# State products in four quarters of TensorE's array, a ScalarE pass moved behind the Squares, and a new order of the first steps

## The chip, the cores and the metric

One core of one Trainium2 chip. The metric is the device time of one execution in microseconds, the median of the runs. The engines that matter here are TensorE (PE in the views, its weight loads PEld), VectorE (DVE), ScalarE (ACT) and the DMA queue that SyncE (SP) feeds.

## The reference

Attention with a decaying state (retention), then two feed-forward layers. q, k, v are (4, 8, 768, 64) in float32; the weights are float64, 512 x 2048 and 2048 x 512 twice.

```python
gamma = 1.0 - 2.0 ** (-5.0 - np.arange(H))
for t in range(S):
    state = gamma * state + k[:, :, t] (outer) v[:, :, t]
    y[:, :, t] = (q[:, :, t] @ state) / sqrt(D)
x = y with heads joined                      # (3072, 512)
h = x @ moe_w_in;   x = (h - tanh(h)) @ moe_w_out
h = x @ moe2_w_in;  out = where(h > 0, h, exp(min(h, 0)) - 1) @ moe2_w_out
```

## The kernel before

**Attention.** The sequence is cut into 6 chunks of 128 positions for each of 4 batches: 24 attention steps s, chunk s // 4 of batch s % 4. Eight heads are four pairs p of two heads j; a head has 64 rows. One attention step has scores (`att_scores`, L164: for each head k against q, 64 rows by 128 columns, j = 0 and j = 1 into two banks, a0 and a1), a mask on VectorE (L172) that gives pt, and a scaling of q in place (`att_scale_q`, L135). Its output (`att_out`) is, for each head, the carried state with the scaled q (the state product, L192: 64 rows by 64 columns) plus v with pt (L200: 128 rows by 64 columns). Both add up in one bank, a0, where head j = 0 of a pair takes partitions 0 to 63 and j = 1 takes 64 to 127. ScalarE copies the output to the high half of x (L208), VectorE subtracts that from the output for the low half (L209). The state's update (`att_state`, `state_mm`, L219: scaled k with v, in bank a1) is added by VectorE (L242, L245). The k for it is scaled on VectorE (`att_scale_k`, L149). The first four attention steps have no state behind them; their updates are copied (L233).

**Feed-forward.** Each product is made of three TensorE passes of high and low halves. The loop runs over steps n = 0 to 191: a block of 512 tokens b and a slice f of 128 of the 2048 inner columns. A step has 12 matmuls into h (`first_mm`, L256), the activation (`act_tanhshrink`, `act_elu`), and 12 matmuls into four accumulators (`second_mm`, L322) for the step two before it (SKEW = 2). An attention step's scores come behind `first_mm` of one step, its output and state behind that of the next; their copies and additions are taken up at the start of the step after that. Those of attention step 5 come at n = 1 and n = 2, of 6 at 3 and 4, of 7 at 5 and 6, and so on, later ones further apart.

**Activation.** On ScalarE: two Squares (L276, L277), `between()`, that is, the hand-over of the previous step's g (`flush`, `split_hi`, L265), Tanh (L279) and Relu (L280). On VectorE four operations (L282, L285, L288, L289), interleaved with a list `side`: the low half of g (L269), masks, and weight passes.

**Weights.** Each float64 tile of 128 x 512 is fetched raw (`fetch`, L81) and made into two float32 halves: `convert_a` on ScalarE (L86) writes a staging tile, one of four (pool `stg`); `convert_b` on VectorE (L93, L94) puts in the missing bits; `convert_c` copies the high half on ScalarE (L106) and subtracts it on VectorE (L107), which frees the staging tile. `todo[n]` names the tiles whose `convert_b` stands in step n; two for each of the first five steps, then one.

The order on every engine is the order in which the program is written (`manual_schedule`); each engine works through its list in turn. Before the loop, a hand-written list of first steps starts the first four attention steps, the first two weight tiles and the scores of attention step 4.

Of the kernel before, what the change touches and what calls it, by code (L numbers as in the profile page):

```python
# [40 lines left out]
def retention_moe_kernel(ctx: ExitStack, tc: tile.TileContext, dims, ins, out):  # L41
# [139 lines left out]

    def att_out(s):
        t, v, _ = qkv_t[s]
        pt = pt_t.pop(s)
        pool, tag = bank(s, "o")
        o = pool.tile([P, NP, P], F32, tag=tag, name=f"o{s}")
        b, c = divmod(s, B)
        if b:
            for p in range(NP):
                for j in range(2):  # L190
                    r = slice(j * D, (j + 1) * D)
                    nc.tensor.matmul(  # L192
                        out=o[r, p, :], lhsT=st[c][r, p, :], rhs=t[r, 0, p * P:(p + 1) * P],
                        start=(p == 0), stop=False, skip_group_check=True,
                    )
        for p in range(NP):
            for j in range(2):
                r = slice(j * D, (j + 1) * D)
                h = 2 * p + j
                nc.tensor.matmul(  # L200
                    out=o[r, p, :], lhsT=v[:, h * D:(h + 1) * D], rhs=pt[:, j, p, :],
                    start=(b == 0), stop=True, skip_group_check=True,
                )
        if c == 0:
            xhl[b] = xp.tile([P, 2, KC, TB], F32R, tag=f"x{b % 2}", name=f"x{b}")
        yield
        sl = slice(c * P, (c + 1) * P)
        nc.scalar.activation(out=xhl[b][:, 0, :, sl], in_=o, func=AF.Copy)  # L208
        nc.vector.tensor_tensor(  # L209
            out=xhl[b][:, 1, :, sl], in0=o, in1=xhl[b][:, 0, :, sl].bitcast(F32), op=ALU.subtract  # L210
        )

    def state_mm(ds, s):
        _, v, kn = qkv_t.pop(s)
        for p in range(NP):
            for j in range(2):
                r = slice(j * D, (j + 1) * D)
                h = 2 * p + j
                nc.tensor.matmul(  # L219
                    out=ds[r, p, :], lhsT=kn[:, h * D:(h + 1) * D], rhs=v[:, h * D:(h + 1) * D],  # L220
                    start=True, stop=True,
                )
# [12 lines left out]
    def att_state(s):  # L235
        if s // B == NCH - 1:
            return
        ds = ps_a.tile([P, NP, D], F32, tag="a1", name=f"ds{s}")
# [138 lines left out]
    def run(g):  # L377
        for _ in g:
            pass
# [4 lines left out]
    with tc.manual_schedule():  # L384
# [41 lines left out]
        def out_pe(s):  # L426
            g_out[s] = att_out(s)
            next(g_out[s])
# [7 lines left out]
        def ops(lst):  # L436
            for op in lst:
                op()
# [7 lines left out]
        convert_a(jobs0[0])  # L446
        run(g_sc[1])
        scores_pe(2)
        run(g_out[0])
        out_pe(1)  # L450
        ops(convert_b(jobs0[0]))
        run(g_sc[2])
        lo0 = convert_c(jobs0[0])
        run(g_out[1])
        scores_pe(3)
        out_pe(2)
        lo0()
        run(g_sc[3])
        run(g_out[2])
        out_pe(3)  # L460
        att_scale_k(0)
        att_scale_k(1)
        run(g_out[3])
        convert_a(jobs0[1])
        att_scale_k(2)
        att_scale_k(3)
# [4 lines left out]
        lo1 = convert_c(jobs0[1])  # L471
# [3 lines left out]
        lo1()  # L475
# [5 lines left out]
        convert_a(jobs0[3])  # L481
        ops(convert_b(jobs0[2]))
        ops(masks4)
        att_scale_k(B)
        ops(convert_b(jobs0[3]))
# [47 lines left out]
        for job in todo[0]:  # L533
            convert_a(job)
# [4 lines left out]
        def flush():  # L539
            if prev_v is not None:  # L540
                g_t[n - 1] = split_hi(prev_v, n - 1)

# [17 lines left out]
        for ph, b, f, flo, fhi in order:  # L560
# [24 lines left out]
            for job in todo.get(n + 1, []):  # L585
                convert_a(job)
# [17 lines left out]
            n += 1  # L604
        flush()
# [62 lines left out]
```

## Time and profile before

| | |
|---|---|
| median of 3 runs | 1172.61 us (1171.87 to 1172.62) |
| the profiled execution, its own time | 1170.16 us |
| its span, first to last instruction | 1168.3 us |
| TensorE busy | 1151.0 us, 99% |
| VectorE busy | 681.2 us, 58% |
| ScalarE busy | 624.1 us, 53% |
| mean granted TensorE clock | 0.995 |

The span is what the trace shows; the execution's own time has some 2 us more around it. A busy share is a mean over the whole span, so it says nothing of a stage: the views by stretch do. In the views an instruction has its line, its engine, what it writes and reads by the program's names, and behind it in brackets how long its engine had been idle and what ended that.

### The profile page before, as it was taken

The numbers are of one execution on the slowest core, as the hardware profiler recorded it, in microseconds if no ns is written. First come the engines' busy times: TensorE is split into PE (matmuls) and PEld (weight loads), VectorE is DVE, ScalarE is ACT, GpSimd is POOL, SyncE is SP. The second block draws the span as 40 slices with busy tenths as digits, with TensorE's granted clock in tenths as the row PEclk, the third lists the DMA queues.
The fourth block names the chain that finished last, engine by engine and source line by source line (L and its number), as shares of the span: only waits on it lengthen the run. The fifth ranks groups of instructions, "written<-read, shape, count | busy, mean of one in ns | idle before, by whom it ended". The sixth has DMA issues, their size and how long they took to land.

```text
span 1168.3 us, 15675 instructions
## 1 busy us (share of the span) xinstructions
PE 1151.0 (99%) x6033; PEld 941.6 (81%) x6033; DVE 681.2 (58%) x1133; ACT 624.1 (53%) x1097; POOL 5.6 (0%) x10
## 2 busy tenths in 40 slices
PE   8799999999999999999999999999999999999998
PEld 5578888888888888888888888888888888888886
DVE  6898887666666666565799766333343343343332
ACT  2657785454455445445788665453443544544434
POOL 0000000000000000000000000000000000000000
PEclk9899999999999999999999999999999999999999
DMA  9930032421103102100565300200200200200000
GB/s 338 415 140 37 1 109 42 139 52 57 37 1 108 37 28 74 45 1 18 191 227 178 108 1 1 72 1 1 73 1 1 73 1 1 73 1 1 36 1 36
DMA packets 27562, 80.44 MB, mean 69 GB/s; under 512 B 3168, under 2 KB 3168, under 8 KB 27488
## 3 DMA queue, kind: packets, MB, share of 16 engines
q1 hardware_dynamic: 26048, 76.56, 18.7%
q0 software_dynamic: 864, 2.10, 1.2%
q8 instruction: 47, 0.77, 0.3%
q10 hardware_dynamic: 576, 0.79, 0.2%
q14 instruction: 27, 0.22, 0.1%
HBM read 64.76 MB, written 14.68 MB: 68 GB/s over the span
## 4 chain that ended last, share of the span: by engine, by line
PE 93%; DVE 3%; ACT 1%; DMA 1%; issue 1%; SPq 0%; DVEq 0%; ACTq 0%
PE acc L322 44%; PE h L256 43%; PE sc L164 2%; PE o L200 2%; PE o L192 1%; PE ds L219 1%; DVE w L94 1%; DMA raw<-w 1%; DVE w L107 1%; DMA stage<-qkv 0%; DVE x L209 0%; DVE v L289 0%; DVE v L285 0%; ACT w L86 0%; DVE h L288 0%
## 5 line engine op out<-in xcount | busy, mean ns | idle before, releaser
L322 PE MATMUL acc<-g,w 128*128 128x512 f32 x1152 | 282.6, 394 | 0.0
L256 PE MATMUL h<-x,w 128*128 128x512 f32 x1152 | 278.6, 391 | 0.0
L322 PE MATMUL acc<-w,g 128*128 128x512 f32 x1152 | 276.7, 389 | 0.6 <-DVE g L269 0.6
L256 PE MATMUL h<-y,w 128*128 128x512 f32 x1152 | 276.7, 389 | 0.0
L256 PEld LDWEIGHTS h<-x,w 128*128 128x128 f32 x1152 | 217.1, 189 | 45.5 <-ACT w L106 0.2
L322 PEld LDWEIGHTS acc<-w,g 128*128 128x128 f32 x1152 | 216.1, 188 | 45.9 <-DVE g L269 1.0
L256 PEld LDWEIGHTS h<-y,w 128*128 128x128 f32 x1152 | 216.2, 188 | 44.9
L322 PEld LDWEIGHTS acc<-g,w 128*128 128x128 f32 x1152 | 213.9, 188 | 47.5 <-ACT g L265 0.7
L302 DVE SCALAR_TENSOR_TENSOR v<-v,t 128x512 f32<-128x512 f32 x96 | 66.5, 693 | 299.6 <-ACT t L300 299.6
L297 ACT ACTIVATE u<-h 128x512 f32<-128x512 f32 x96 | 57.4, 598 | 259.8 <-PE h L256 258.3
L276 ACT ACTIVATE u<-h 128x512 f32<-128x512 f32 x96 | 57.5, 599 | 224.7 <-issue 216.0
L282 DVE SCALAR_TENSOR_TENSOR v<-v,u 128x512 f32<-128x512 f32 x96 | 66.4, 692 | 152.7 <-ACT v L277 152.6
L269 DVE TENSOR_TENSOR g<-v,g 128x512 fp32r<-128x512 f32 x192 | 131.4, 685 | 0.8 <-ACT g L265 0.8
L265 ACT ACTIVATE g<-v 128x512 fp32r<-128x512 f32 x192 | 118.0, 615 | 2.0 <-DVE v L305 2.0
L289 DVE COPY_PREDICATED v<-m,h 128x512 f32<-128x512 uint16 x96 | 70.4, 734 | 4.5
L277 ACT ACTIVATE v<-u,qa_b 128x512 f32<-128x512 f32 x96 | 69.4, 723 | 3.2
L280 ACT ACTIVATE m<-u,xs_b 128x512 bf16<-128x512 f32 x96 | 68.1, 710 | 0.0
L288 DVE TENSOR_TENSOR h<-h,t 128x512 f32<-128x512 f32 x96 | 66.5, 692 | 0.0
L305 DVE TENSOR_TENSOR v<-h,v 128x512 f32<-128x512 f32 x96 | 65.6, 683 | 0.0
L285 DVE SCALAR_TENSOR_TENSOR v<-v,h 128x512 f32<-128x512 f32 x96 | 65.4, 681 | 0.0
L298 ACT ACTIVATE v<-u 128x512 f32<-128x512 f32 x96 | 60.7, 632 | 3.1
L300 ACT ACTIVATE t<-u 128x512 f32<-128x512 f32 x96 | 59.2, 617 | 0.0
(44 smaller groups left out, 601.6 us busy)
## 6 DMA issues: line engine op xcount, KB each, us to landing
raw<-w SPq DMA_DIRECT2D x64, 512.0 KB, 5.6
qk<-qkv SPq DMA_DIRECT2D x20, 512.0 KB, 5.3
v<-qkv SPq DMA_DIRECT2D x24, 256.0 KB, 5.8
x<-x1d SPq DMA_DIRECT2D x12, 512.0 KB, 5.8
kn<-qkv SPq DMA_DIRECT2D x20, 256.0 KB, 5.9
out<-o SPq DMA_DIRECT2D x10, 512.0 KB, 2.9
x1d<-o SPq DMA_DIRECT2D x8, 512.0 KB, 3.3
stage<-qkv SPq DMA_DIRECT2D x4, 512.0 KB, 6.8
```

The lines of the kernel that those rows point to most:

```text
L256: nc.tensor.matmul(out=h, lhsT=w[:, a, c * P:(c + 1) * P], rhs=x[:, b, c, :], start=(i == 0), stop=(i == 3 * KC - 1),)
L265: nc.scalar.activation(out=t[:, 0, :], in_=g, func=AF.Copy)
L269: nc.vector.tensor_tensor(out=t[:, 1, :], in0=g, in1=t[:, 0, :].bitcast(F32), op=ALU.subtract)
L277: nc.scalar.activation(out=v, in_=u, func=AF.Square, bias=qa_b)
L280: nc.scalar.activation(out=big, in_=u, func=AF.Relu, bias=xs_b)
L282: lambda: nc.vector.scalar_tensor_tensor(out=v, in0=v, scalar=QB, in1=u, op0=ALU.add, op1=ALU.mult),
L285: lambda: nc.vector.scalar_tensor_tensor(out=v, in0=v, scalar=C2, in1=h, op0=ALU.mult, op1=ALU.mult),
L288: lambda: nc.vector.tensor_tensor(out=h, in0=h, in1=th, op=ALU.subtract),
L289: lambda: nc.vector.copy_predicated(out=v, mask=big.bitcast(U16), data=h),
L302: lambda: nc.vector.scalar_tensor_tensor(out=v, in0=v, scalar=1.0, in1=th, op0=ALU.add, op1=ALU.mult),
L305: lambda: nc.vector.tensor_tensor(out=v, in0=h, in1=v, op=ALU.max),
L322: nc.tensor.matmul(out=acc[e], lhsT=lhsT, rhs=rhs, start=(f == lo and i == 0), stop=(f == hi - 1 and i == 2),)
```

## The change

It does three things. The state products of an odd pair p go to the other half of the partitions of the output (`half`), so that heads change places there, and the output has two tiles, even pairs in bank a0 and odd pairs in a1, with the update of the state in the rest of a1; the copies to x are made for each tile, and the rows of the first weight are exchanged on the host to match. `convert_a` is called inside `between()`, behind the hand-over of g, and for the tiles of the same step; it was called at the end of the step before. And the list of first steps has another order.

```diff
--- before.py
+++ after.py
@@ -179,36 +179,54 @@
         else:
             yield masks + [lambda: att_scale_q(s)]
 
+    def half(p, j):
+
+
+        j = (j + p) % 2
+        return slice(j * D, (j + 1) * D)
+
+    ds_t = {}
+
     def att_out(s):
         t, v, _ = qkv_t[s]
         pt = pt_t.pop(s)
-        pool, tag = bank(s, "o")
-        o = pool.tile([P, NP, P], F32, tag=tag, name=f"o{s}")
         b, c = divmod(s, B)
-        if b:
+        if b == 0:
+            pool, tag = bank(s, "o")
+            o = pool.tile([P, NP, P], F32, tag=tag, name=f"o{s}")
+            outs = [o[:, p, :] for p in range(NP)]
+            parts = [(slice(0, NP), o)]
+        else:
+            even = ps_a.tile([P, NP // 2, P], F32, tag="a0", name=f"oe{s}")
+            odd = ps_a.tile([P, NP, P], F32, tag="a1", name=f"oo{s}")
+            ds_t[s] = odd[:, NP // 2:, :].rearrange("p a (b d) -> p (a b) d", d=D)
+            outs = [(even, odd)[p % 2][:, p // 2, :] for p in range(NP)]
+            parts = [(slice(0, NP, 2), even), (slice(1, NP, 2), odd[:, 0:NP // 2, :])]
             for p in range(NP):
                 for j in range(2):
                     r = slice(j * D, (j + 1) * D)
                     nc.tensor.matmul(
-                        out=o[r, p, :], lhsT=st[c][r, p, :], rhs=t[r, 0, p * P:(p + 1) * P],
-                        start=(p == 0), stop=False, skip_group_check=True,
+                        out=outs[p][half(p, j)], lhsT=st[c][r, p, :], rhs=t[r, 0, p * P:(p + 1) * P],
+                        start=(p < 2), stop=False, skip_group_check=True,
                     )
         for p in range(NP):
             for j in range(2):
-                r = slice(j * D, (j + 1) * D)
                 h = 2 * p + j
                 nc.tensor.matmul(
-                    out=o[r, p, :], lhsT=v[:, h * D:(h + 1) * D], rhs=pt[:, j, p, :],
+                    out=outs[p][half(p, j)], lhsT=v[:, h * D:(h + 1) * D], rhs=pt[:, j, p, :],
                     start=(b == 0), stop=True, skip_group_check=True,
                 )
         if c == 0:
             xhl[b] = xp.tile([P, 2, KC, TB], F32R, tag=f"x{b % 2}", name=f"x{b}")
         yield
         sl = slice(c * P, (c + 1) * P)
-        nc.scalar.activation(out=xhl[b][:, 0, :, sl], in_=o, func=AF.Copy)
-        nc.vector.tensor_tensor(
-            out=xhl[b][:, 1, :, sl], in0=o, in1=xhl[b][:, 0, :, sl].bitcast(F32), op=ALU.subtract
-        )
+        x = xhl[b]
+        for k, o in parts:
+            nc.scalar.activation(out=x[:, 0, k, sl], in_=o, func=AF.Copy)
+        for k, o in parts:
+            nc.vector.tensor_tensor(
+                out=x[:, 1, k, sl], in0=o, in1=x[:, 0, k, sl].bitcast(F32), op=ALU.subtract
+            )
 
     def state_mm(ds, s):
         _, v, kn = qkv_t.pop(s)
@@ -218,7 +236,7 @@
                 h = 2 * p + j
                 nc.tensor.matmul(
                     out=ds[r, p, :], lhsT=kn[:, h * D:(h + 1) * D], rhs=v[:, h * D:(h + 1) * D],
-                    start=True, stop=True,
+                    start=True, stop=True, skip_group_check=True,
                 )
 
     def att_state_pair(j):
@@ -235,7 +253,7 @@
     def att_state(s):
         if s // B == NCH - 1:
             return
-        ds = ps_a.tile([P, NP, D], F32, tag="a1", name=f"ds{s}")
+        ds = ds_t.pop(s)
         state_mm(ds, s)
         c = s % B
         yield
@@ -443,45 +461,44 @@
         warm(3)
         run(g_sc[0])
         out_pe(0)
-        convert_a(jobs0[0])
         run(g_sc[1])
         scores_pe(2)
         run(g_out[0])
+        convert_a(jobs0[0])
         out_pe(1)
+        run(g_sc[2])
+        scores_pe(3)
+        run(g_out[1])
+        out_pe(2)
+        run(g_sc[3])
         ops(convert_b(jobs0[0]))
-        run(g_sc[2])
-        lo0 = convert_c(jobs0[0])
-        run(g_out[1])
-        scores_pe(3)
-        out_pe(2)
-        lo0()
-        run(g_sc[3])
         run(g_out[2])
         out_pe(3)
+        lo0 = convert_c(jobs0[0])
         att_scale_k(0)
-        att_scale_k(1)
         run(g_out[3])
+        lo0()
         convert_a(jobs0[1])
-        att_scale_k(2)
-        att_scale_k(3)
+        for s in range(1, B):
+            att_scale_k(s)
         pairs = [att_state_pair(j) for j in range(2)]
         for g in pairs:
             next(g)
         ops(convert_b(jobs0[1]))
-        lo1 = convert_c(jobs0[1])
         convert_a(jobs0[2])
         for g in pairs:
             run(g)
-        lo1()
+        lo1 = convert_c(jobs0[1])
         att_load_v(B)
         att_load_kn(B)
         for job in jobs0[4:12]:
             fetch(*job)
         masks4 = next(att_scores(B))
-        convert_a(jobs0[3])
         ops(convert_b(jobs0[2]))
+        lo1()
         ops(masks4)
         att_scale_k(B)
+        convert_a(jobs0[3])
         ops(convert_b(jobs0[3]))
 
 
@@ -530,8 +547,6 @@
 
         pend = []
         prev_jobs = jobs0[2:4]
-        for job in todo[0]:
-            convert_a(job)
         load_step(load.pop(-1))
         gens = []
         prev_v = None
@@ -539,6 +554,8 @@
         def flush():
             if prev_v is not None:
                 g_t[n - 1] = split_hi(prev_v, n - 1)
+            for job in jobs:
+                convert_a(job)
 
         def second(upto):
             while len(pend) > upto:
@@ -582,8 +599,6 @@
             interleave(chain, side)
             if n in scale_k:
                 att_scale_k(scale_k[n])
-            for job in todo.get(n + 1, []):
-                convert_a(job)
             prev_v = v
             prev_jobs = jobs
             pend.append((2 * ph + 1, f, n, b, flo, fhi))
@@ -602,6 +617,7 @@
                 if 8 <= f < 8 + KC:
                     split_x1(nxt, f - 8)
             n += 1
+        assert not jobs
         flush()
         split_lo(g_t[n - 1], prev_v)
         second(0)
@@ -632,6 +648,9 @@
     }
     for m, w in enumerate((moe_w_in, moe_w_out, moe2_w_in, moe2_w_out)):
         w = np.asarray(w)
+        if m == 0:
+            w = w.reshape(KC, 2, P // 2, DFF).copy()
+            w[1::2] = w[1::2, ::-1].copy()
         if m % 2 == 0:
             w = w.reshape(KC, P, NF, P).transpose(2, 1, 0, 3).reshape(NF, P, KC * P)
         else:
```

On TensorE, at step n = 2, the output of attention step 5 (o5 is its tile, oe5 and oo5 are the tiles of even and odd pairs), between `first_mm` and `second_mm`. Before:

```order
L256 MATMUL h0_2_506<-x0_190,w0_2_413 128x512 x12
L192 MATMUL o5_519<-qk5_357,st0_284 64x128 x8
L200 MATMUL o5_519<-pt5_454,v5_431 64x128 x8
L219 MATMUL ds5_536<-v5_431,kn5_359 64x64 x8
L322 MATMUL acc0_0_574<-g0_471,w1_0_415 128x512 x3
```

And now:

```order
L274 MATMUL h0_2_504<-x0_190,w0_2_413 128x512 x12
L208 MATMUL oe5_517<-qk5_353,st0_284 64x128 x2
L208 MATMUL oo5_518<-qk5_353,st0_284 64x128 x2
L208 MATMUL oe5_517<-qk5_353,st0_284 64x128 x2
L208 MATMUL oo5_518<-qk5_353,st0_284 64x128 x2
L215 MATMUL oe5_517<-pt5_452,v5_427 64x128 x2
L215 MATMUL oo5_518<-pt5_452,v5_427 64x128 x2
L215 MATMUL oe5_517<-pt5_452,v5_427 64x128 x2
L215 MATMUL oo5_518<-pt5_452,v5_427 64x128 x2
L237 MATMUL oo5_518<-v5_427,kn5_355 64x64 x8
L340 MATMUL acc0_0_572<-g0_469,w1_0_415 128x512 x3
```

The eight state products keep their place and their number; they now go by twos to either tile, and so do the products with v.

On ScalarE, step n = 2 and the start of n = 3: u, v, g, t and m are tiles of the activation, w32 the staging tiles, w the weights, x the input of the first layer. Before:

```order
L86 ACTIVATE w32_0_5_494<-raw0_5_324 128x512
L86 ACTIVATE w32_1_3_496<-raw1_3_326 128x512
L276 ACTIVATE u2_545<-h0_2_506 128x512
L277 ACTIVATE v2_547<-u2_545,qa_b_91 128x512
L265 ACTIVATE g1_551<-v1_467 128x512
L279 ACTIVATE t2_546<-h0_2_506 128x512
L280 ACTIVATE m2_548<-u2_545,xs_b_92 128x512
L106 ACTIVATE w0_4_555<-w32_0_4_427 128x512
L106 ACTIVATE w1_2_557<-w32_1_2_429 128x512
L86 ACTIVATE w32_0_6_570<-raw0_6_328 128x512
L86 ACTIVATE w32_1_4_572<-raw1_4_330 128x512
L208 ACTIVATE x1_395<-o5_519 128x4x128
L276 ACTIVATE u3_624<-h0_3_600 128x512
```

And now:

```order
L294 ACTIVATE u2_543<-h0_2_504 128x512
L295 ACTIVATE v2_545<-u2_543,qa_b_91 128x512
L283 ACTIVATE g1_549<-v1_465 128x512
L86 ACTIVATE w32_0_5_551<-raw0_5_323 128x512
L86 ACTIVATE w32_1_3_553<-raw1_3_325 128x512
L297 ACTIVATE t2_544<-h0_2_504 128x512
L298 ACTIVATE m2_546<-u2_543,xs_b_92 128x512
L106 ACTIVATE w0_4_557<-w32_0_4_471 128x512
L106 ACTIVATE w1_2_559<-w32_1_2_473 128x512
L225 ACTIVATE x1_392<-oe5_517 128x2x128
L225 ACTIVATE x1_392<-oo5_518 128x2x128
L294 ACTIVATE u3_624<-h0_3_600 128x512
```

The two passes over raw weights stood ahead of the output's copy (o5) and of the first Square of step 3; now the passes of step 2 stand behind the hand-over of g and ahead of Tanh, and the copy, now in two, stands behind the high halves of step 1's weights.

On VectorE, in the list of first steps: pt are masked scores of attention steps 0 to 3, w32_0_0 is the first weight tile. Before:

```order
L209 TENSOR_TENSOR x0_190<-o0_181,x0_190 128x4x128
L93 TENSOR_SCALAR w32_0_0_191<-w32_0_0_191 128x512
L94 SCALAR_TENSOR_TENSOR w32_0_0_191<-raw0_0_128,w32_0_0_191 128x512
L172 TENSOR_TENSOR pt2_195<-sc2_0_196,dtab_88 128x512
L172 TENSOR_TENSOR pt2_195<-sc2_1_197,dtab_88 128x512
L209 TENSOR_TENSOR x0_190<-o1_208,x0_190 128x4x128
L107 TENSOR_TENSOR w0_0_221<-w32_0_0_191,w0_0_221 128x512
L172 TENSOR_TENSOR pt3_225<-sc3_0_226,dtab_88 128x512
L172 TENSOR_TENSOR pt3_225<-sc3_1_227,dtab_88 128x512
L209 TENSOR_TENSOR x0_190<-o2_236,x0_190 128x4x128
L149 TENSOR_TENSOR kn0_137<-kn0_137,ktab_89 128x512
L149 TENSOR_TENSOR kn1_139<-kn1_139,ktab_89 128x512
```

And now:

```order
L227 TENSOR_TENSOR x0_190<-o0_181,x0_190 128x4x128
L172 TENSOR_TENSOR pt2_193<-sc2_0_194,dtab_88 128x512
L172 TENSOR_TENSOR pt2_193<-sc2_1_195,dtab_88 128x512
L227 TENSOR_TENSOR x0_190<-o1_208,x0_190 128x4x128
L172 TENSOR_TENSOR pt3_219<-sc3_0_220,dtab_88 128x512
L172 TENSOR_TENSOR pt3_219<-sc3_1_221,dtab_88 128x512
L93 TENSOR_SCALAR w32_0_0_206<-w32_0_0_206 128x512
L94 SCALAR_TENSOR_TENSOR w32_0_0_206<-raw0_0_128,w32_0_0_206 128x512
L227 TENSOR_TENSOR x0_190<-o2_232,x0_190 128x4x128
L149 TENSOR_TENSOR kn0_137<-kn0_137,ktab_89 128x512
L227 TENSOR_TENSOR x0_190<-o3_247,x0_190 128x4x128
L107 TENSOR_TENSOR w0_0_256<-w32_0_0_206,w0_0_256 128x512
```

The two bit operations of the first weight tile stood ahead of the masks of attention step 2; now they stand behind those of step 3, and the tile's last pass behind the fourth output.

## Rows read from the trace of the kernel before

**Rows 1.** Waits, whole run, TensorE: who waited, for whom, us in total, times, longest.
```profile
PE sc L164 <- DVE x L209: 7.4, 3, 3.5
...
PE acc L322 <- DVE g L269: 0.6, 1, 0.6
```

**Rows 2.** Busy us (instructions) of PE, PEld, DVE, ACT, POOL by stretch; PEclk, DMA share, GB/s.
```profile
26.40:77.50 51.10, 42.91 (x302) 33.90 (x301) 44.47 (x81) 30.20 (x53) 0.00 (x0) 0.90 0.84 339
77.50:1168.30 1090.80, 1086.69 (x5509) 893.78 (x5508) 621.35 (x1026) 586.56 (x1034) 5.42 (x6) 1.00 0.16 50
...
37.80:44.60 6.80, 6.13 (x24) 4.94 (x25) 6.70 (x13) 3.69 (x7) 0.00 (x0) 0.50 1.03 414
...
72.00:76.30 4.30, 3.19 (x14) 2.19 (x13) 3.57 (x8) 2.68 (x5) 0.00 (x0) 1.00 0.00 0
```

**Rows 3.** Waits of VectorE and ScalarE from 26.4 to 77.5 us.
```profile
DVE v L282 <- ACT v L277: 3.2, 3, 1.4
DVE x L209 <- ACT x L208: 3.0, 3, 1.2
...
ACT w L86 <- DVE w L107: 19.0, 5, 5.1
```

**Rows 4.** Timeline of step 1: start us, us, engine, line, operation, idle before and its end.
```profile
35.88 1.26 ACT L86 ACTIVATE w<-raw 128x512 f32<-128x512 f32 x2 [2.92 <-DVE w L107]
37.04 0.58 ACT L208 ACTIVATE x<-o 128x512 fp32r<-128x512 f32 x1
...
37.66 0.69 DVE L209 TENSOR_TENSOR x<-o,x 128x512 fp32r<-128x512 f32 x1 [1.21 <-ACT x L208]
...
38.40 2.93 PE L164 MATMUL sc<-qk 64*128 64x128 f32 x16 [3.51 <-DVE x L209]
```

**Rows 5.** Timeline, VectorE, steps 0 to 5: the other idle spells.
```profile
30.86 0.69 DVE L282 SCALAR_TENSOR_TENSOR v<-v,u 128x512 f32<-128x512 f32 x1 [0.45 <-ACT v L277]
...
49.13 0.69 DVE L282 SCALAR_TENSOR_TENSOR v<-v,u 128x512 f32<-128x512 f32 x1 [1.39 <-ACT v L277]
...
74.77 0.69 DVE L209 TENSOR_TENSOR x<-o,x 128x512 fp32r<-128x512 f32 x1 [0.63 <-ACT x L208]
```

**Rows 6.** Timeline, TensorE and VectorE, start of the program.
```profile
13.70 1.16 PE L164 MATMUL sc<-stage 64*128 64x128 f32 x16 [0.55 <-DMA stage<-qkv]
...
14.44 0.42 DVE L93 TENSOR_SCALAR w<-w 128x512 uint32<-128x512 uint32 x1
...
14.79 1.09 PE L200 MATMUL o<-pt,v 128*64 128x128 f32 x16
...
26.86 1.28 DVE L172 TENSOR_TENSOR pt<-sc,dtab 128x512 f32<-128x512 f32 x2
```

**Rows 7.** Groups by line, whole run: count, busy us, mean ns of one.
```profile
L245 DVE TENSOR_TENSOR st<-ds,st 128x256 f32<-128x256 f32 x16 | 6.8, 425 | 1.7
```

**Rows 8.** SyncE's load of step 1's q and k: timeline row, and its landing.
```profile
27.50 0.33 SPq L125 DMA_DIRECT2D qk<-qkv  x1
...
DMA to landing us min/median/max: 10.4/10.4/10.4
```

**Rows 9.** Timeline, TensorE: small products, dense stage first, then the start.
```profile
179.69 1.09 PE L192 MATMUL o<-qk,st 64*64 64x128 f32 x16
180.71 1.09 PE L200 MATMUL o<-pt,v 128*64 128x128 f32 x16
...
224.79 0.43 PE L192 MATMUL o<-qk,st 64*64 64x128 f32 x4
...
18.77 0.43 PE L200 MATMUL o<-pt,v 128*64 128x128 f32 x2 [0.77 <-DVE pt L172]
19.37 1.09 PE L200 MATMUL o<-pt,v 128*64 128x128 f32 x14 [0.16 <-DVE pt L172]
20.57 1.29 PE L219 MATMUL dsp<-v,kn 128*64 128x64 f32 x32
```

**Rows 10.** Groups by line, TensorE, from 77.5 us on.
```profile
L192 PE MATMUL o<-qk,st 64*64 64x128 f32 x272 | 18.5, 275 | 0.0
```

## Prediction

> **What bounds it now.** Read the waits of TensorE first: over the whole run it waits 7.4 us, three times, for VectorE's copy of an attention output (L209), and after 77.5 us only once, 0.6 us [rows 1]. Then the busy times by stretch: from 77.5 us to the end TensorE is busy for 1086.69 of 1090.80 us, while VectorE and ScalarE have 621.35 and 586.56 us of work there; from 26.4 to 77.5 us it is busy for 42.91 of 51.10 us [rows 2]. So there are two stages. In the late one a microsecond taken off TensorE's own work is a microsecond of the end; a microsecond of ScalarE or VectorE is nothing. In the early one (steps n = 0 to 5) TensorE waits, and the question is for whom.
>
> The waits of that stretch say: VectorE idles 3.2 us for the second Square (L277) and 3.0 us for the copy L208, three times each; ScalarE idles 19.0 us in `convert_a` (L86) for VectorE's last pass over an older weight tile (L107), whose staging buffer it wants [rows 3]. The timeline of step 1 shows the ring: L86 starts at 35.88 us after 2.92 us of waiting for L107, L208 stands behind it at 37.04, L209 waits 1.21 us for that, and the scores of TensorE wait 3.51 us for L209 [rows 4]. VectorE is otherwise packed there, so TensorE arrives where VectorE's queue lets it: VectorE's idle time is what can be won.
>
> **The change, part by part.**
>
> *`convert_a` behind the second Square.* It takes L86 from in front of L208 and of the Squares and puts it, with the hand-over of g, ahead of Tanh and Relu. VectorE's idle spells are 0.45 (step 0), 1.21 (step 1), 1.39 (step 2), 1.21 (step 3, a row like that of step 1), 1.39 (step 4, like step 2) and 0.63 us (step 5): 6.2 us in all, as the totals say [rows 3 to 5]. The 0.45 stays: there the Squares wait for TensorE's h, not for L86. The other 5.8 should go, because L107 is no longer waited for ahead of L208 and of the Squares. What is late next: Tanh, now behind L86. I followed step 2 through the new queues with these durations: L107 of the buffer's last owner ends about 45.8 us, the two L86 at 47.1, Tanh at 47.6; VectorE wants Tanh about 49.2, so 1.6 us cover it. In steps 3 and 5 the second Square would end within 0.1 us of when VectorE asks for it; each may give back 0.2 us or so. In the late stage L86 is covered by the skew of two steps between a weight tile's passes and its use.
>
> *The order of the first steps.* VectorE does the same operations up to the copies of the first states, in another order. Before, the two bit operations of the first weight tile (the first at 14.44 us) fill a time in which the next mask could not run yet: its scores start at 13.70 and take 1.16 us [rows 6]. After, they stand behind the fourth mask. VectorE then waits about 0.45 us for those scores and 0.5 us for ScalarE's copy of the second output (its products start at 14.79 and take 1.09 us; a copy takes 0.58 [rows 4]), and catches up part of it later. Stepped through, the masks of the fifth attention step start at about 27.6 instead of 26.86 us [rows 6]: a loss of 0.7 us. Bounds: 0, if the waits are absorbed, and 1.0, if none is. The queues of SyncE and GpSimd keep their order; no DMA is moved past another.
>
> *The outputs in two halves.* Each later attention step copies two half tiles twice instead of one tile. A 256-wide VectorE operation takes 425 ns against 0.69 us for L209 [rows 4, 7]; two cost 0.16 us more by that, about 0.08 as they overlap in the queue. Three stand ahead of the last early wait: 0.2 us. In the late stage nothing, there is room on both engines [rows 2].
>
> *Step 1.* Its scores also need q and k of that step, issued at 27.50 us and landing 10.4 us later, at 37.9 [rows 8]. In the new chain the first bank is free at about 37.5 and the second (state added) at 38.6, so the load ends that wait first and TensorE still idles some 2.6 us. The granted clock was 0.50 (1.2 GHz) over the stretch 37.8 to 44.6 us, from within the 3.51 us of idling on, and full (2.4 GHz) over 72.0 to 76.3 us, with 1.11 us of idling [rows 2, 4]; 2.6 lies between. If it falls, scores and h of step 1 and 2 take up to twice as long, some 3 us; VectorE's queue (packed until about 47 us) hides all but about 0.5. I take 0 and keep 0.5 for the range.
>
> Early sum: 5.8 - 0.7 - 0.2 = **4.9 us** (3.5 to 5.8 with the bounds). The outputs of steps 0, 2 and 4 win nothing more there by faster products: what follows them waits for VectorE's k (L149).
>
> *State products in four quarters.* An attention output has eight products of a state (L192), each in two passes: 16 matmuls in 1.09 us; four take 0.43, so a pair more costs (1.09 - 0.43)/6 = 0.11 us [rows 9]: two run side by side, rows 0-63 to columns 0-63 and rows 64-127 to 64-127. The change sends odd products to the other half of the columns and to another bank, so that all four quarters have work. No row shows four at once. For it: products that share all rows but not the columns (L200) keep the same 1.09 us for 16, and products that share columns but not rows (L164) 1.16 [rows 6], so neither sharing slows a pair. And a product need not wait for its turn: where the mask held up the second product, two passes ran alone in 0.43 us, and the 14 left then took 1.09 us, as long as 16 do: eight slots, six of two and two of one, since the left half had three products to go and the right one four [rows 9]. The halves keep queues of their own; with quarters this gives 4 slots instead of 8, 4 x 0.11 = 0.44, less 0.01 for two more starts: **0.43 us**. Bounds: 0, if no more than two ever run; 0.24, if matmuls can't come closer than L219's 32 in 1.29 us, 0.04 each, so that a slot of four takes 0.16 (8 x 0.11 - 4 x 0.16) [rows 9]; above, 0.44. I take 0.43, since each kind of sharing has its row. There are 272/16 = 17 outputs after 77.5 us [rows 10], all in the dense stage: 17 x 0.43 = **7.3 us**. The products with v (L200) come in the column order 0, 1, 1, 0; by the same queues they keep eight slots. States' updates (L219) are unchanged but for their bank.
>
> The Trainium skill, "TensorE: Matmul & The Clock Gate" (Part 3, "What overlaps and what doesn't"), says that a weight load overlaps a running matmul only where the row group differs, and that matmuls start strictly in order. By that a quarter that shares rows with a running one waits, the term is 0, and the time is that of the first rival below. This trace disagrees: L200's two column halves share all rows and pair as L192's do, and the 14 matmuls above passed a second pass that was still waiting [rows 9].
>
> Sum: 4.9 + 7.3 = 12.2 us. The profiled execution took 1170.16 us, so 1158.0 on its account; the median of the runs is 1172.61, 2.45 higher, and the prediction is made for that: **1160.4 us**.
>
> **The rivals.**
> *No more than two at once.* Everything else as above: 1172.6 - 4.9 = 1167.7 us. For it: no row of four. Against: the rows of either sharing, and of the separate queues.
> *The early win is lost.* Another wait takes the place of the ring, Tanh behind L86, or the 2.6 us of idling and a clock at 1.2 GHz through step 2 and on, and VectorE's idle time stays: 1172.6 - 7.3 = 1165.3 us. For it: the margins of 0.1 us in steps 3 and 5. Against: 1.6 us at Tanh.
> *Slower: quarters that take turns.* If two row halves writing the same columns into two banks, with two column halves reading the same rows, make each matmul run alone, 16 slots replace 8: 0.88 us more for each of 17 outputs, 15.0, less the early 4.9: 1182.7 us. It decides from 4.9/17 = 0.29 us an output. For it: no row has both sharings together. Against: each alone costs nothing.
>
> **How the numbers follow.** Forecast 0.62, two at once 0.18, early win lost 0.12, turns 0.05, and 0.03 for both gains near nothing, within 0.2%. A measurement can tell about 0.2%, 2.3 us, from no change; the first three lie beyond it. Faster 0.90 (some of the first three may shrink below it, so not 0.92), same 0.04, slower 0.06. The range: the forecast's own goes from 1172.6 - 5.8 - 7.5 = 1159.3, less 2.45 for the lower account of the profiled execution, about 1157, to 1172.6 - 3.5 - 17 x 0.24 = 1165.0; up to 1168.5 it takes in the second rival and most of the first. Outside are the turns, and the first rival where the early win is small too.
>
> **What would show it.** State products: 16 in about 0.65 us instead of 1.09, and the products with v 0.6 instead of 1.02 us after their start. No wait of L86 for L107 ahead of the copy, VectorE's waits in the early stretch about 1 us instead of 6.2. TensorE still idles some 8 us there, now also for q and k of its attention steps (L135, L149), at full clock. The scores of step 5 done by about 72.5 us (before: 77.5, where the dense stage begins). First h products 0.7 us later than before. Wrong if state products keep 1.09 us, if the scores of step 5 end after 75, or if TensorE waits anywhere after them.

## The result and the profile after

The change takes 1162.25 us (median, 1160.70 to 1164.14), the kernel before 1172.24 (1170.98 to 1172.62): a ratio of 0.9918 [0.9904, 0.9932], 10.0 us less. The forecast was 12.2 us less, at 1160.4. The profiled execution of the change took 1164.14 us, the slowest of its runs; that of the kernel before took 1170.16, 2 us below its median. The two traces are therefore 6.0 us apart where the medians are 10.0 apart, and what they lack is in the early stage.

The lines of the kernel have moved: in the change the Squares are L294 and L295, Tanh is L297, and VectorE's four operations of the activation are L300, L303, L306 and L307 (before: L282, L285, L288, L289); the copies of an output are L225 and L227, the products L208, L215, L237, and the states L251 and L263. In the runs with Tanh first, further down, the four operations stand one line lower still.

TensorE's waits over the whole run, for [rows 1] (who waited, for whom, us in total, times, longest):

```profile
PE sc L164 <- DVE x L227: 4.4, 3, 3.0
PE sc L164 <- DMA stage<-qkv: 3.7, 3, 2.1
PE dsp L237 <- DVE kn L149: 2.4, 2, 1.3
...
PE sc L164 <- DVE st L263: 2.0, 3, 0.7
...
PE oo L237 <- DVE kn L149: 1.0, 2, 0.6
...
PE acc L340 <- DVE g L287: 0.6, 1, 0.6
```

The stages, cut where the last early scores end (77.96 us; 77.46 before), for [rows 2], and two stretches of the early one in which the granted clock was 0.50 (1.2 GHz):

```profile
26.40:77.96 51.56, 44.18 (x326) 34.50 (x322) 47.12 (x88) 30.54 (x57) 0.00 (x0) 0.88 0.89 348
77.96:1162.40 1084.44, 1079.63 (x5509) 886.55 (x5508) 624.64 (x1043) 588.69 (x1052) 5.42 (x6) 1.00 0.16 50
...
24.90:31.70 6.80, 6.51 (x57) 5.61 (x54) 6.64 (x12) 1.19 (x2) 0.00 (x0) 0.50 0.92 349
41.90:48.70 6.80, 6.22 (x25) 4.96 (x26) 6.73 (x14) 2.28 (x5) 0.00 (x0) 0.50 1.04 418
```

The dense stage went from 1090.84 us (77.46 to 1168.30) to 1084.44, 6.4 less; by the medians that leaves 3.6 us for the early stage, where 4.9 was forecast. In this execution the early stage even ends 0.5 us later than before: what the ring (L86 waiting for L107's staging tile) had cost is gone, and something else took it up. VectorE's waits from 26.4 to 78 us, for [rows 3]:

```profile
DVE v L303 <- ACT t L297: 2.1, 4, 0.7
DVE v L300 <- ACT v L295: 2.1, 1, 2.1
```

The 19.0 us of L86 for L107 and the 3.0 us of the copies are gone, and so are the waits for the second Square except one, in step 0. In their place VectorE's second operation of the activation (L303) waits for Tanh. Step 2 shows how (start us, us, engine, line, operation, idle before and its end):

```profile
51.58 1.23 ACT L86 ACTIVATE w<-raw 128x512 f32<-128x512 f32 x2
...
52.71 0.58 ACT L297 ACTIVATE t<-h 128x512 f32<-128x512 f32 x1
...
53.32 0.69 DVE L303 SCALAR_TENSOR_TENSOR v<-v,h 128x512 f32<-128x512 f32 x1 [0.70 <-ACT t L297]
```

L303 doesn't use Tanh's result; it reads h, which Tanh reads too, and the program has it wait until Tanh is done (53.29 us). Tanh now stands behind the two raw passes.

The first output of the dense stage, for [rows 9], on TensorE:

```profile
83.64 0.33 PE L208 MATMUL oe<-qk,st 64*64 64x128 f32 x2
83.66 0.33 PE L208 MATMUL oo<-qk,st 64*64 64x128 f32 x2
83.80 0.28 PE L208 MATMUL oe<-qk,st 64*64 64x128 f32 x2
83.82 0.28 PE L208 MATMUL oo<-qk,st 64*64 64x128 f32 x2
...
84.02 0.28 PE L208 MATMUL oe<-qk,st 64*64 64x128 f32 x2
84.03 0.28 PE L208 MATMUL oo<-qk,st 64*64 64x128 f32 x2
84.24 0.33 PE L215 MATMUL oe<-pt,v 128*64 128x128 f32 x2
```

Four quarters run at once: two to `oe` and two to `oo` start within 20 ns, and each next four 0.11 to 0.16 us behind. The products with v follow 0.60 us after the first state product, in all 20 outputs 597 or 598 ns; before it was 1020 or 1021. That is 0.423 us an output, and 17 outputs make 7.2 us. The dense stage gained 0.8 us less than that, most of it at one place: the state's update of attention step 8 now comes before its k is scaled (the view ends behind the twelfth of its 16 matmuls).

```profile
182.14 0.57 PE L237 MATMUL oo<-v,kn 128*64 128x64 f32 x12 [0.48 <-DVE kn L149]
```

So the quarters did what was forecast. What fell short is for the most part in the early stage, and the experiments take the three parts of the change apart.

### The profile page after: what moved, and what is told of

Read it like the earlier page. It is cut to its first block, busy times and chain, and to the rows that moved or that the text cites. A ratio compares the mean times of both kernels' runs of the same rounds, so it can differ in the third digit from the quotient of the medians.

```text
span 1162.4 us, 15704 instructions
## 1 busy us (share of the span) xinstructions
PE 1142.7 (98%) x6033; PEld 934.3 (80%) x6033; DVE 684.9 (59%) x1153; ACT 625.2 (54%) x1117; POOL 5.6 (0%) x10
## 4 chain that ended last, share of the span: by engine, by line
PE 94%; DVE 3%; DMA 2%; issue 0%; SPq 0%; ACT 0%; DVEq 0%; ACTq 0%
PE acc L340 45%; PE h L274 44%; PE sc L164 2%; PE oe L215 1%; PE oe L208 1%; PE oo L237 1%; PE oo L215 1%; DMA raw<-w 1%; DMA stage<-qkv 1%; DVE w L94 1%; DMA dtab<-dtab 1%; DVE w L107 1%; DVE kn L149 0%; DVE v L307 0%; SPq L81 0%
## 5 line engine op out<-in xcount | busy, mean ns | idle before, releaser
L274 PE MATMUL h<-x,w 128*128 128x512 f32 x1152 | 279.7, 392 | 0.0
L274 PE MATMUL h<-y,w 128*128 128x512 f32 x1152 | 276.7, 389 | 0.0
L274 PEld LDWEIGHTS h<-x,w 128*128 128x128 f32 x1152 | 218.0, 190 | 45.9 <-issue 0.4
L274 PEld LDWEIGHTS h<-y,w 128*128 128x128 f32 x1152 | 216.2, 188 | 44.9
L294 ACT ACTIVATE u<-h 128x512 f32<-128x512 f32 x96 | 57.6, 600 | 236.8 <-issue 224.8
L300 DVE SCALAR_TENSOR_TENSOR v<-v,u 128x512 f32<-128x512 f32 x96 | 66.4, 692 | 137.1 <-ACT v L295 137.1
L307 DVE COPY_PREDICATED v<-m,h 128x512 f32<-128x512 uint16 x96 | 70.4, 733 | 4.5
L303 DVE SCALAR_TENSOR_TENSOR v<-v,h 128x512 f32<-128x512 f32 x96 | 65.6, 683 | 10.0 <-ACT t L297 10.0
L295 ACT ACTIVATE v<-u,qa_b 128x512 f32<-128x512 f32 x96 | 69.5, 724 | 3.1
L306 DVE TENSOR_TENSOR h<-h,t 128x512 f32<-128x512 f32 x96 | 66.5, 692 | 0.0
```

The lines of the kernel that those rows point to most:

```text
L274: nc.tensor.matmul(out=h, lhsT=w[:, a, c * P:(c + 1) * P], rhs=x[:, b, c, :], start=(i == 0), stop=(i == 3 * KC - 1),)
L295: nc.scalar.activation(out=v, in_=u, func=AF.Square, bias=qa_b)
L300: lambda: nc.vector.scalar_tensor_tensor(out=v, in0=v, scalar=QB, in1=u, op0=ALU.add, op1=ALU.mult),
L303: lambda: nc.vector.scalar_tensor_tensor(out=v, in0=v, scalar=C2, in1=h, op0=ALU.mult, op1=ALU.mult),
L306: lambda: nc.vector.tensor_tensor(out=h, in0=h, in1=th, op=ALU.subtract),
L307: lambda: nc.vector.copy_predicated(out=v, mask=big.bitcast(U16), data=h),
```

## The experiments

Each time is a median with the lowest and highest run; "before" is the kernel before, run beside it on the same chip. "The list" is the hand-written order of the first steps.

### One part at a time

**The quarters alone.** The change, with the raw passes back in their old place and the old list of first steps:

```diff
-            for job in jobs:
-                convert_a(job)
...
+            for job in todo.get(n + 1, []):
+                convert_a(job)
```

> The kernel before with the state products in quarters, the two output tiles and the halved copies alone; passes over raw weights and the order of the first steps as before. Theory: the quarters account for 0.42 us of each of the 17 outputs in the dense stage, and nothing of the early stage moves: 7.2 us less than before, about 1165.0 us, products with v 0.60 us behind the state products' start. Rival (the quarters' gain is partly given back by the second pair of copies on VectorE, which is full in the early stage): 6 us less or worse, and the last scores of the early stage later than 77.5 us.

1164.51 us (1163.65 to 1166.67), before 1172.11: 0.9942 [0.9929, 0.9954], 7.6 less; the term was 7.3. VectorE's early waits are still those behind L86, for the Square and for the copy (2.35 of the 5.1 us are in step 0, where L86 waits for its raw tile and not for L107):

```profile
DVE v L300 <- ACT v L295: 5.1, 3, 2.3
DVE x L227 <- ACT x L225: 2.4, 3, 1.0
```

**The raw passes alone**, in the kernel before:

```diff
             g_t[n - 1] = split_hi(prev_v, n - 1)
+            for job in jobs:
+                convert_a(job)
...
-            for job in todo.get(n + 1, []):
-                convert_a(job)
```

> The kernel before with the passes over raw weights behind the hand-over of g alone. Theory: the ring of waits goes (5.8 us of VectorE's idle time), but Tanh, now behind two raw passes, is late for VectorE's second operation of the activation, which reads h as Tanh does: about 2 us come back, so 3 to 4 us less than before, about 1168.6 us, VectorE waiting for Tanh some 2 us before 78 us. Rival (the early win was lost to the first steps' order and the clock, not to Tanh): 5 us less or more, about 1167 us. Second rival (nothing is won, the ring's waits only change their name): within 1 us of before.

1166.84 us (1166.21 to 1168.71), 0.9963 [0.995, 0.9975], 5.3 less; the term was up to 5.8. The expectation that Tanh would take some 2 us back missed, and its rival (5 us less or more) came out: the 2.7 us that VectorE waits for Tanh here are not lost to the end one for one. The ring is gone, and Tanh is there:

```profile
DVE v L285 <- ACT t L279: 2.7, 4, 1.2
DVE pt L172 <- PE sc L164: 1.7, 1, 1.7
DVE v L282 <- ACT v L277: 0.6, 2, 0.5
```

**The start order alone**, in the kernel before: the hand-written list of the change, nothing else.

```diff
         out_pe(0)
-        convert_a(jobs0[0])
...
         run(g_out[0])
+        convert_a(jobs0[0])
...
         run(g_sc[3])
+        ops(convert_b(jobs0[0]))
```

> The kernel before with the new order of the first steps alone. Theory of the prediction: VectorE reaches the masks of the fifth attention step 0.7 us later, and since VectorE is full until step 5, the end is 0.7 us later: 1172.9 us. Rival (the new order lets TensorE idle longer ahead of the third scores, and a clock at 1.2 GHz adds to that): 2 to 3.5 us slower, 1174 to 1176 us, first h products after 28 us. Second rival (the new order helps, as the copies come earlier): up to 1 us faster.

1172.62 us (1170.80 to 1174.43), 1.0004 [0.9995, 1.0013]: 0.5 us slower, no difference that can be told from none (the interval goes from 0.6 us faster to 1.5 slower).

**All but the start order**: the change with the old list.

> The changed kernel with the old order of the first steps (quarters and raw passes remain). Theory: 7.2 from the quarters and 3 to 4 from the raw passes: about 1161.5 us, 0.7 less than the changed kernel. Rival (the new order of the first steps took 3 us): about 1159 us. Second rival (the order does not matter): 1162.3 us, as the changed kernel.

1160.18 us (1159.20 to 1161.60), 0.9901 [0.9886, 0.9916]: 11.9 less, and 2.1 below the change, more than the 0.7 expected. So the new list costs at most 1.5 us, and perhaps nothing, where the ring stands (L86 waits 19.0 us for L107 with the new list alone too), and about 2 us where the ring is gone. The last early scores end at 73.48 us.

### Why the new list costs more than 0.7 us

The change was run again on another chip (before 1172.06), as the base of what follows.

> The changed kernel once more, unaltered, beside the next two on one chip. Theory (the order of the first steps costs, with the quarters and the raw passes beside it, about 2 us): 1162 us again, the early stage's last scores 2 us later in the median than with the old order. Rival (the 2 us between the changed kernel and the one with the old order lay in the runs: the clock fell twice ahead of the first h products in the one profiled execution): 1161 us or less, within 0.7 us of the kernel with the old order, and a profiled execution that has its first h products by 27.5 us.

1162.83 us (1162.11 to 1163.81), 0.9925 [0.9912, 0.9937]; last early scores at 76.43. VectorE's waits from 9 to 31 us, in this run:

```profile
DVE pt L172 <- PE sc L164: 2.6, 2, 1.7
DVE x L227 <- ACT x L225: 1.6, 2, 1.1
```

and with the old list:

```profile
DVE x L227 <- ACT x L225: 1.7, 2, 1.2
DVE pt L172 <- PE sc L164: 1.5, 2, 0.8
DVE v L300 <- ACT v L295: 0.5, 1, 0.5
```

VectorE waits 1.1 us more for scores (2.6 against 1.5) and hardly less for the copies (1.6 against 1.7): the two bit operations (L93, L94) that filled this time are elsewhere. The masks of the fifth attention step start at 27.81 us in the one and 26.62 in the other. A second thing comes with it, the granted clock. From 23 to 31 us, with the scores of the fifth attention step (L164) and the first h products (L274), the change run again and then the old list:

```profile
23.00:31.00 8.00, 7.64 (x68) 6.55 (x65) 7.80 (x15) 1.87 (x3) 0.00 (x0) 0.57 0.94 353
...
25.52 2.67 PE L164 MATMUL sc<-qk 64*128 64x128 f32 x16 [0.36 <-DVE st L251]
28.12 3.97 PE L274 MATMUL h<-x,w 128*128 128x512 f32 x12
```

```profile
23.00:31.00 8.00, 6.91 (x90) 5.52 (x90) 7.45 (x14) 3.49 (x6) 0.00 (x0) 1.00 0.98 372
...
24.49 1.75 PE L164 MATMUL sc<-qk 64*128 64x128 f32 x16 [0.98 <-DVE st L251]
26.18 3.01 PE L274 MATMUL h<-x,w 128*128 128x512 f32 x12
```

The granted clock fell to 0.50 (1.2 GHz) between 23.4 and 27.0 us in all six profiled executions with the new list, and in none of the seven with the old. In the change run again TensorE was busy for 1.03 us of the stretch from 20 to 23, with the old list for 2.26; that the idle time is what brings the clock down is argued from this, not shown. The scores start 1.0 us later, and scores and h products together take 1.9 us longer at that clock, so h is done 2.9 us later; VectorE's wait for the second Square of step 0 is 2.1 us instead of 0.5, and the early stage ends 2.95 us later (76.43 against 73.48). By these two traces, one of each kernel, the lowered clock takes more of it than the order ahead of the masks.

**The k scalings together.** One theory was that k's scalings, now behind the weight's low half, hold up the updates and so the clock; the rival, that the masks come late whatever follows them.

```diff
         att_scale_k(0)
+        att_scale_k(1)
         run(g_out[3])
-        lo0()
         convert_a(jobs0[1])
-        for s in range(1, B):
+        for s in range(2, B):
             att_scale_k(s)
+        lo0()
```

> The changed kernel with one piece of the first steps' old order back: the scalings of k stand together again ahead of the state updates (the first two before the fourth output's copy, the first weight tile's low half behind all four). Theory (in the new order the first state updates wait 1.17 and 1.25 us for k, TensorE's clock falls to 1.2 GHz about 24 us and the fifth scores and first h products take 1.8 us longer): waits for k of about 0.6 us, no fall of the clock ahead of 37 us, first h products by 27.5 us, and 1 to 2 us less than the changed kernel, about 1161 us. Rival (the masks' order costs, VectorE idling for the third scores): the waits for k shrink, but the end stays within 0.7 us of the changed kernel, 1162.5 us.

1163.11 us (1161.63 to 1163.98), before 1171.17, 0.9932 [0.9918, 0.9946]: 0.3 above the change run again, though on another chip. TensorE's waits for k ahead of the first updates only shrank, from 2.4 to 1.7 us in all, though it is busy here for 2.09 us of the stretch from 20 to 23; and the clock still falls, at 27.0 us. So the k scalings alone don't explain the fall of the clock. Its cost was not tried: here too the first h products run at 1.2 GHz (4.60 us). The order ahead of the masks and the clock both stay as causes, and no run moves the bit operations alone or holds the clock up there.

### Tanh behind the raw passes

The raw passes (`raws`, no longer in `between`) move behind Tanh; only Relu follows them there, whose result VectorE needs for the last of its four operations alone.

```diff
         between()
         nc.scalar.activation(out=th, in_=h, func=AF.Tanh)
+        raws()
```

> The changed kernel with the raw passes one place further back, behind Tanh. Theory (Tanh behind two raw passes makes VectorE wait some 2 us before 78 us): VectorE no longer waits for Tanh, 1 to 2 us less than the changed kernel. Rival (that wait lies where VectorE would wait for something else): within 0.5 us of the changed kernel.

1160.63 us (1159.18 to 1161.13), before 1172.06, 0.9904 [0.9891, 0.9918]: 2.2 below the change run again, and no wait for Tanh is left in VectorE's waits from 26.4 to 78 us:

```profile
DVE v L301 <- ACT v L295: 2.7, 3, 2.1
DVE w L93 <- ACT w L86: 0.3, 1, 0.3
```

**With the old list as well.**

> Raw passes behind Tanh and the old order of the first steps, with the quarters. Theory: 1 to 2 us less than the 1160.2 us of the kernel with the old order alone, about 1158.7 us, the fastest of all. Rival: 1160 us as that one, since q and k of step 1 land too late for more.

1159.24 us (1159.01 to 1159.65), 0.9894 [0.9879, 0.9909]. It was run once more on a third chip, beside the last two runs of this document:

> Raw passes behind Tanh and the old order of the first steps once more, as the measure of the run with the products of zeros and as a second look at the fastest so far. Theory: 1159.2 us again, 3.5 us less than the changed kernel. Rival (the first time was luck of the runs): 1160.2 us or more.

1159.09 us (1158.07 to 1159.58), 0.9895 [0.9881, 0.9908]. This is the fastest version: 12.1 to 12.8 us below the kernel before, 3.0 to 3.7 below the change, and its eight runs lie between 1158.07 and 1159.65. By it the list is worth 1.4 us where Tanh comes first (1160.63 to 1159.24), and Tanh's place 0.9 with the old list (1160.18 to 1159.24); these 0.9 are not clear of the runs' spread, since two of the four runs with Tanh behind the raw passes (1159.20 and 1159.50) lie among the eight.

### The quarters' queues

State products by pair in the order 0, 2, 1, 3: pairs 0 and 2 want the same two quarters, so the first four of the eight products (eight matmuls, as each has two passes) now stand ahead of those for the other two quarters.

```diff
-            for p in range(NP):
+            for p in (0, 2, 1, 3):
```

> The changed kernel with the state products in the order of pairs 0, 2, 1, 3, so that the first four products want only two of the quarters. Theory (each quarter has a queue of its own, and a product does not wait for one ahead of it that wants another quarter): 0.60 us from the first state product to the products with v, as in the order 0, 1, 2, 3. Rival (TensorE looks only a product or two ahead): the first four go by twos and the last four by twos, 1.02 us. Between the two, where the look ahead ends: 0.7 to 0.8 us.

One run, 1164.59 us. The state products of one output, as sums of one stretch (us, PE, PEld, PEclk, DMA share, GB/s), in this order:

```profile
83.83:84.44 0.61, 0.61 (x16) 0.44 (x16) 1.00 0.00 0
```

and in the change:

```profile
83.64:84.24 0.60, 0.60 (x16) 0.43 (x16) 1.00 0.00 0
```

13 ns more (611, in one output 615, against 598 from the first state product to the first product with v). The first matmul to `oo` has eight to `oe` ahead of it in the program, and starts 0.03 us behind the first of them, before the other six have started:

```profile
33.67 0.33 PE L208 MATMUL oe<-qk,st 64*64 64x128 f32 x2
33.70 0.33 PE L208 MATMUL oo<-qk,st 64*64 64x128 f32 x2
33.83 0.28 PE L208 MATMUL oe<-qk,st 64*64 64x128 f32 x2
```

So a matmul whose quarter is taken does not hold up those of other quarters behind it, as if each quarter had a queue of its own; here TensorE does not work through its list in turn.

### The idle time of step 1

With the ring gone and the old list TensorE waits for q and k of step 1, and the clock falls behind it:

```profile
PE sc L164 <- DMA qk<-qkv: 3.7, 1, 3.7
```

Twelve products of zeros behind the h products of step 1 fill most of that wait, in the fastest version (`zt`, the zeros, has a buffer of its own for it):

```diff
             h = first_mm(2 * ph, xhl[ph * NB + b], f, n)
+            if n == 1:
+                zp = ps_acc.tile([P, TB], F32, tag="acc0", name="warmq")
+                for _ in range(12):
+                    nc.tensor.matmul(out=zp, lhsT=zt[:, 0:P], rhs=zt, start=True, stop=True)
```

> Raw passes behind Tanh and the old order of the first steps, plus twelve products of zeros on TensorE in step 1 behind its h products, where it idles 3 to 5 us for q, k and VectorE. Theory (VectorE sets the pace there, the clock only adds): the clock stays at 2.4 GHz, the h products of step 2 take 2.9 instead of 4.8 us, and the end moves by 0 to 1 us less than without them. Rival (the fall of the clock in step 1 costs its whole 3 us): 2.5 us less or more. Second rival (the extra products come in the way of the scores): up to 1 us more.

1159.94 us (1157.76 to 1160.54), 0.99 [0.9886, 0.9913], against 1159.09 without: nothing gained, with runs on both sides of those without. From 34 to 49 us, with the zero products and then without:

```profile
34.00:49.00 15.00, 11.29 (x97) 7.81 (x97) 14.97 (x29) 11.20 (x22) 0.00 (x0) 1.00 1.03 410
```

```profile
34.00:49.00 15.00, 11.23 (x85) 8.63 (x84) 14.85 (x28) 9.17 (x19) 0.00 (x0) 0.77 1.02 412
```

The clock stays full, and h of step 2 takes 3.04 us instead of 4.91; but VectorE is busy for 14.85 of 15 us already, and the last early scores end at 71.81 instead of 72.27. VectorE sets the pace there, not TensorE's clock.

## Why the prediction was right or wrong

**The quarters: right.** 0.423 us an output where 0.43 was taken; the quarters alone gave 7.6 us for 7.3. Between the Trainium skill and the rows it went as the rows had it: as the prediction read "TensorE: Matmul & The Clock Gate" (Part 3, "What overlaps and what doesn't") of the Trainium skill, the second quarter on the same rows would wait, and four ran at once (16 matmuls in 0.60 us). In the traces 0.8 us of this term were lost in the dense stage, most of it to a wait that "if TensorE waits anywhere after them" had named without a price: the update of step 8 waits 0.48 us for k, with no slack left in front of it.

**The raw passes: the ring right, "1.6 us cover it" wrong.** The waits for L86 went as said, and alone the move gave 5.3 us. But the step "VectorE wants Tanh about 49.2" fits the operation that uses Tanh's result, the third (L288); the second (L285, L303 now) already waits for Tanh, since both read h. With the old list VectorE is ready for it at 48.15 us, and Tanh ends at 48.81 instead of 47.6, because the Squares wait until 45.31 for h of step 2, which ran at 1.2 GHz. It costs VectorE 2.1 to 2.7 us over the early steps, and the time 2.2 us with the new list (1162.83 to 1160.63) and perhaps 0.9 with the old. The rival "the early win is lost" had the right wait in it, and the prediction set it aside by the wrong operation.

**The start order: half of the mechanism, and the size off.** The term was 0.7 with an upper bound of 1.0, for the case that none of the waits is absorbed. It can't be told from 0 alone, and is 2.1 us in the company of the other parts (2.6 by the second run of the change). What the bound left out: VectorE's wait for scores grew by 1.1 us and none of it was caught up, so that the fifth step's masks are 1.2 us later; and the clock fell ahead of the first h products, which the prediction looked for in step 1 alone, so that these ended 2.9 us later instead of 0.7. In its own account the early sum reads 5.8 - 0.9 (Tanh) - 2.1 (start order) instead of 5.8 - 0.7 - 0.2, some 2 us less, which is the difference between 12.2 and 10.0. That the sum closes is no proof of each term: the 0.9 is within the spread, the 5.8 was measured as 5.3 alone, and the 0.2 for the halved copies was not separated.

**Step 1: right without the new list.** TensorE waits there for q and k (5.7 us with the raw passes alone, 3.9 with the old list, 3.7 in the fastest version; 2.6 was said), and the clock falls; taken at 0, it costs nothing that can be seen in the run with zero products. In the change itself q and k are there first: TensorE waits 3.0 us for VectorE's last pass over the output (L227), which is late by the early delay. That these waits pass at full clock was wrong.

**The signs.** The scores of step 5 were to be done by about 72.5 us, with 75 as the sign of being wrong: they end at 77.96 and 76.43 us in the two profiled executions of the change, at 73.48 with the old list and 72.27 in the fastest version. VectorE's early waits were to be about 1 us: they are 4.2 in the change, 2.9 with the old list, 1.4 in the fastest version. So two of the three signs of being wrong came up, in the scores and in the wait of step 8, and the time still comes near the forecast because the quarters carry most of the sum. The early forecast nearly holds for the quarters and the raw passes together, not for the three parts. The masks of the fifth attention step vary from one execution to the next: 27.2 to 29.6 us in the six with the new list, 26.5 to 28.0 in the seven with the old. The traces show what goes with it. From 12 to 20 us, the profiled execution of the change and then the change run again:

```profile
12.00:20.00 8.00, 6.07 (x66) 5.18 (x66) 3.92 (x7) 1.81 (x4) 0.00 (x0) 0.79 1.00 375
```

```profile
12.00:20.00 8.00, 5.73 (x80) 4.72 (x80) 5.44 (x10) 2.53 (x5) 0.00 (x0) 1.00 1.00 371
```

In four of the thirteen profiled executions the granted clock was at 0.50 (1.2 GHz) from 14.6 to 14.9 us on to 18.0 to 18.3 already, and these have the latest masks of their list: 29.35 to 29.59 us in three with the new list, against 27.2 to 28.1 in the other three, and 28.01 in one with the old, against 26.5 to 26.9 in the other six. The profiled execution of the change is one of the four and took 1.9 us more than the median, and that of the kernel before took 2.1 us less than its own; so these two traces show none of the early win while the medians do. That the clock makes the masks late is argued from this, and why it falls there in some executions only was not tried.

## What to carry to other kernels

When work is moved ahead of an instruction, look for every instruction on other engines that waits for it, not for those alone that use its result: a second reader of the same tile can be bound to its order too. A term that is measured in a kernel with a stall in it need not be the term without the stall: the start order cost nothing that could be told from none alone (0.5 us) and about 2 us once the ring had gone, so a part is to be priced in the company it will have. And where an operation filled a gap on a busy engine, moving it out leaves the gap.

## What the runs showed of the hardware

Four 64 x 64 quarters of the array run products side by side, 16 matmuls of 128 columns in 0.60 us against 1.02 with two at a time, though quarters share rows and columns; out of order over the pairs it is 0.61. The granted clock fell to 0.50 (1.2 GHz) between 23.4 and 27.0 us in every profiled execution with the new list and in none with the old; keeping it at 1.00 in step 1 with zero products, in the version with the old list, did not shorten the time where VectorE was the bound (1159.94 against 1159.09 us).
